# Two more staging buffers in the last projection stage, and a new order of GpSimd's and VectorE's work around the gate and up products

## The chip, the cores and the metric

The kernel runs on one core of one Trainium2 chip. Its time is the device time of one execution in microseconds (us); the time of a kernel is the median of its runs. The profile is one further execution, recorded by the hardware profiler. Its rows use these names: PE is TensorE's matmuls and PEld its weight loads, DVE is VectorE, ACT is ScalarE, POOL is GpSimd, SP is SyncE; SPq, ACTq and POOLq are the queues on which these engines issue transfers (DMA). `L115` is line 115 of the kernel before.

## The reference

The input x has 2048 rows of 640 columns. It is normalised by rows, goes through a local attention and, beside it, through a gated feed-forward without activation, and the two are joined:

```python
xn = _layernorm(x, axis=-1)
# attention: 32 heads of 20, each position looks at 8 positions, 2 apart, to its left
qkv = (xn @ wqkv)...
logits = einsum("bhsd,bhswd->bhsw", q, kg) * scale   # masked where the position is negative
o = einsum("bhsw,bhswd->bhsd", softmax(logits), vg)
s = o.reshape(B, S, D) @ wo
# feed-forward: 640 -> 1536 -> 640
h = (xn @ w_gate) * (xn @ w_up)
g = silu(h @ w_down)
out = x + s * g
```

All of it is float32.

## The kernel before

**Precision.** Each float32 operand of a matmul is held as two parts, a high part (ScalarE copies the value to the matmul's rounded type, L114) and a low part (value minus high part, L115, on GpSimd or VectorE; L1168, L829 and L975 are the same step elsewhere). Every product is the sum of three: high by high, high by low, low by high (`ALL3`). `split` makes both parts.

**Stages.** The text of the program is one long list, unrolled; each engine works through its own instructions in the order in which they stand, and waits where an operand isn't there or a buffer isn't free.

1. Normalise and transpose x into `xT`, four pieces of 512 rows (tag `xc`), high and low part.
2. Queries, keys and values. `qkv` (L434) makes one tile of 128 rows with 15 matmuls, in one of three PSUM banks in turn (`q`, `g`, `u`); ScalarE copies it to a staging buffer (L448), and after every second tile ScalarE's queue stores the buffer to DRAM (L452, `qkv_scr`). The heads are made in five passes (`MADE`); the last has 16 tiles, n = 0 to 15. `staged` holds three staging buffers: two halves of one slot `y` and one buffer `pk`; after n = 9 (`NT - 7`) the buffer `pk` leaves the list, because the high and low parts of the gate weights (`G`) go there next.
3. The attention itself runs on VectorE (L542, L549, L508 and the softmax, L564 to L578), GpSimd (the sums L514) and a little ScalarE, in the background of stages 2 and 4. It is a generator: `advance(budget)` adds to a credit, and steps of the attention are written into the program as long as the credit is positive, each at an assumed cost. In stage 4 the budget of a product is the number of its matmuls times `GROUP_RATE`. Finished heads are stored to `o_scr` (L590).
4. Gate and up. The 1536 columns of the two weights make 12 pieces f = 0 to 11 of 128. Pieces 1 to 11 are made in `group`: a 2 x 2 block scheme with seven products instead of eight, for two row pieces (`c0` and `c0 + 1`) and for gate and up at once. I write 1H, 2H and so on for `group(f, 2)`, the upper half of the rows, and 2L, 3L, ... for `group(f, 0, 1)` or, for f = 11, `group(f1)`, the lower half. The order is 1H, 2H, 2L, 3H, 3L, ..., 10H, 10L, 11L; the upper half of f = 11 follows as plain products (`gate` and `up`, L124).
5. The output projection, the down projection and the join.

**One group.** The seven products stand in the order j = 0, 5, 2, 1, 4, 3, 6 (steps n = 0 to 6) with 6, 9, 6, 9, 6, 9, 9 matmuls (L1310). A product reads one weight unit and one row unit. The weight units lie in four tiles that exist once: `G` (the gate: A11, A12 and a fifth, steps 0 and 1), `S` (the sums S1 to S3, steps 2, 3 and 4), `R` (S4 and the difference d5, step 5, and rows 3 to 5, which the split `U` fills: the up weight's A22, step 6, and its fifth, the last three matmuls of step 3 and of step 6). So, while group f runs, the tiles for f + 1 are written one after the other as their last readers finish: `w_add` makes the sums S1, S2, S3, S4, d5 on GpSimd (L1256), and `w_split` splits G, S, R, U (L114 on ScalarE, L115 on GpSimd). The dictionaries `one_places` (for f = 1) and `two_places` say at which step each of these stands: the key is (0 or 1 for the half, n). The raw weights come by `load_wf` (`wraw`, L180).

Row units named T1 to T4 are sums and differences of `xT`. Those for the upper half are made in stage 2. Those for the lower half were made early and stored; `load_t(0)` to `load_t(3)` (L1149, `t_scr`, 768 KB each) bring back four tiles of them. In the order of the units, T1 lies in tiles 0 and 1, T2's high part in tile 1, T2's low part in tile 2, T3 in tiles 2 and 3. T4 is written into the first rows of `xT` itself by `load_e` (L1153, `e_scr`, 512 KB each); `load_e(3, 0, 2)` and `load_e(3, 1, 3)` put the high and the low part of `xT[3]` back for the plain products of f = 11. All these transfers are issued by GpSimd, in the order of its instructions.

**The end of a group.** `hold(j)` (L1279, ScalarE) copies the bank after steps 0, 2, 3 and 4 (j = 0, 2, 1, 4) to tiles `gh`; the bank of j = 0, 2, 4, 6 is one and goes on accumulating, as does the bank of j = 1 and 3, so the next product on a bank waits for the copy. Then `gate_a` (L1292), `gate_b` (L1282) and `up_a` (L1295) on VectorE and `up_b` (L1285) and `h_b` (L1288) on `eng` finish gate and up and multiply them. `eng` is VectorE for the upper half from f = 2 on, and GpSimd otherwise. `gate_b` and `up_b` stand behind step 6's matmuls; `up_a` and `h_b` stand in `unfinished`, which the next group empties after its step 0 (`finish_piece`). The results are stored by SP (`store_h`, L1268).

**The last group.** The dictionary `beside` puts the first work of the output projection between the steps of 11L: `turn_pair(0)` (L725, L952 to L955), `hi_pair` (L971) and `lo_pair` (L975). After it come `gate(f1, 2)`, `up(f1, 2)`, `gate(f1, 3)`, `up(f1, 3)`. `up(f1, 2)` writes the bank that 11L used for j = 0, 2, 4, 6, so it waits for `up_a`.

Of the kernel before, what the change touches and what calls it, by code (L numbers as in the profile page):

```python
# [44 lines left out]
PACE = 1.0  # L45
VEC = 2
EARLY = 1
GROUP_RATE = 0.184


def tile_column(s):
# [5 lines left out]
def kernel(  # L57
# [702 lines left out]
    def wd_sum(n):  # L760

        t = {name: w_scr[:, i] for i, name in enumerate(("T1", "T2", "T3", "T4"))}
        if n == 0:
            for name, b in (("T1", "B11"), ("T3", "B12"), ("T2", "B22"), ("T4", "B21")):
                nc.sync.dma_start(t[name], wd_block(b))
        else:
            out, y = ((t["T1"], wd_block("B12")), (t["T3"], wd_block("B22")), (t["T2"], t["T1"]), (t["T4"], t["T2"]))[n - 1]
            nc.gpsimd.dma_start(out, y, accum_op=ALU.add)
# [188 lines left out]
    def hi_pair(p, part):  # L957

        if part == 2:
            z, raw = slot([P, 2, 3 * KS, P]) if p else blocks(w_big[0], 1, 2, 3 * KS), pair_raw[p]  # L960
        else:
            raw = pair_y[p][:, part]
            if p < 2:
                z = blocks(w_big[3], 3 + 2 * part, 2, KD) if p else blocks(w_kv["T2"], 1 + 2 * part, 2, KD)
            elif part == 0:
                z = blocks(w_big[p % 2], 2, 2, KD)
            else:
                z = slot([P, 2, KD, P]) if p % 2 else st([P, 2, KD, P], "pk", 1, F32R)
        z = [z[:, i] for i in range(2)]
        pair_z[p, part] = z, raw  # L970
        nc.scalar.activation(z[0], raw, AF.Copy)  # L971

    def lo_pair(p, part):
        z, raw = pair_z[p, part]
        nc.vector.tensor_sub(z[1], raw, z[0].bitcast(F32))  # L975
# [170 lines left out]
    def load_t(n):  # L1146

        tt[0].append(slot([P, 3, CH]))
        nc.gpsimd.dma_start(tt[0][n], t_scr[:, 3 * n:3 * n + 3])  # L1149

    def load_e(ch, a, n):

        nc.gpsimd.dma_start(xT[ch][a][:, 0:2, :], e_scr[n])  # L1153
# [93 lines left out]
    def w_add(f, *names):  # L1247

        if f not in w_sum:
            w_sum[f] = st([P, 9, P], "wraw", 2)  # L1250
        r, t = wf_raw[f], w_sum[f]
        v = {"A11": r[:, 0:2, 0], "A12": r[:, 2:4, 0], "A21": r[:, 0:2, 1], "A22": r[:, 2:4, 1], "g5": r[:, 4, 0],
             "u5": r[:, 4, 1], "S1": t[:, 0:2], "S2": t[:, 2:4], "S3": t[:, 4:6], "S4": t[:, 6:8], "d5": t[:, 8]}
        for name in names:
            a, b = W_SUM[name]
            nc.gpsimd.tensor_tensor(v[name], v[a], v[b], op=ALU.add if name == "S1" else ALU.subtract)  # L1256
# [14 lines left out]
    def group(f, c0=0, second=0):  # L1271

        b = {"A": pt([P, CH], "g", 2), "C": pt([P, CH], "u", 2), "B": q_one}
        kept, later = {}, []
        eng = nc.vector if c0 and f >= VEC else nc.gpsimd

        def hold(j):
            kept[j] = st([P, CH], "gh", 5)
            nc.scalar.activation(kept[j], b["ACACABA"[j]], AF.Copy)  # L1279

        def gate_b():
            nc.vector.tensor_add(kept[2], kept[2], b["C"])  # L1282

        def up_b():
            eng.tensor_add(kept[1], kept[1], kept[4])  # L1285

        def h_b():
            eng.tensor_mul(kept[2], kept[2], kept[1])  # L1288
            store_h(f, c0 + 1, kept[2])

        def gate_a():
            nc.vector.tensor_add(kept[0], kept[0], b["B"])  # L1292

        def up_a():
            nc.vector.tensor_mul(kept[0], kept[0], b["A"])  # L1295
            store_h(f, c0, kept[0])

        if not second:
            if not two(f - 1):
                w_split(f, "U")  # L1300
            w_sum.pop(f, None)
            wf_raw.pop(f)
        for n, j in enumerate((0, 5, 2, 1, 4, 3, 6)):
            y = b["ACACABA"[j]]
            runs = [(w_unit(f, H_IN[j], k)[i], x_in(W_IN[j], l, k, c0)) for i, l in ALL3 for k in range(2)]
            if j in FIVE:
                name, ch = FIVE[j]
                runs += [(w_unit(f, name)[i], xT[c0 + ch][l][:, KD - 1, :]) for i, l in ALL3]
            for r, (w, x) in enumerate(runs):
                nc.tensor.matmul(y, w, x, start=j in (0, 1, 5) and r == 0, stop=r == len(runs) - 1,  # L1310
                                 skip_group_check=True)
            if j in (0, 1, 2, 4):
                hold(j)
            finish_piece()
            if n == 6 and (second, n) in places and (second or f == F_TWO):
                places.pop((second, n))(f)
            for act in later:
                act()
            later = {5: [gate_a], 3: [gate_b, up_b]}.get(j, [])
            if j == 6:  # L1320
                unfinished.extend([up_a, h_b])
            if (second, n) in places:
                places[second, n](f)
            if (f, second, n) in beside:
                beside[f, second, n]()
            if (second, n) == (0, 0) and f < f1 and f + 1 not in wf_raw:
                load_wf(f + 1)
            advance(PACE * len(runs) * (GROUP_RATE if two(f) else 0.184))
# [38 lines left out]
        yield  # L1367

    steps += [differences(k) for k in range(2)]
    paced = 0.0  # L1370
    last, BLOCK = len(MADE) - 1, (3, 4, 6, 8, 10)
    W_SUMS = ((1, 2), (1, 12), (2, 4), (2, 12), (3, 7))
    RATE = ((1.0, 0.4), (0.3, 0.2), (0.4, 0.6), (0.8, 0.8))
    for m, t in ((m, t) for m in range(1, len(MADE)) for t in range(DIL)):
        r = t if m < last else DIL - 1 - t
        begin_unit(m, r)
        heads, broad = MC[m] // DH, m < last and MC[m + 1] > CMAX
        for i in range(NE):
            n = t * NE + i
            if 1 < m < last and n == 0:  # L1380
                load_wq(m + 1, ((0, 3), (3, 5)))
            if m < last and n in BLOCK:
                split_wq(m + 1, nc.gpsimd, (BLOCK.index(n), BLOCK.index(n) + 1))
            elif broad and n == BLOCK[1] + 1:
                load_wq(m + 1, ((4, 5),))
            if (m, r, i) == (last - 1, 1, 6):
                load_wf(F_TWO)
            if (m, n) in W_SUMS:
                wd_sum(W_SUMS.index((m, n)))
            qkv(m, r, i)  # L1390
            if m == last and n == NT - 7:
                staged[:] = [y for y in staged if y is not stage_pk[-1]]
            elif m == last and n == NT - 5:
                load_t(0)
            elif m == last and n == NT - 3:
                w_split(F_TWO, "G")
            if i == 1:
                finish_piece()
            advance(PACE * heads * 0.38)
            paced += RATE[m - 1][t]  # L1400
            while paced >= 1:
                paced -= 1
                step()
        if (m, r) == (last - 1, 1):
            steps.append(first_parts())
        elif (m, r) == (last, 1):
            for k in range(2):
                last_difference(k)
# [13 lines left out]
    def sums(*names):  # L1422
        return lambda f: w_add(f + 1, *names)

    def splits(*names):
        return lambda f: w_split(f + 1, *names)
# [2 lines left out]
                  (1, 2): splits("G"), (1, 4): splits("S"), (1, 5): splits("R"), (1, 6): splits("U")}  # L1429

    def load_late(n):
        if n == 0:
            load_t(1)
            load_t(2)
        elif n == 1:
            load_t(3)
        else:
            load_e(1, 0, 0)
            load_e(1, 1, 1)

    one_places = {(0, 1): sums("S1", "S2"), (0, 2): sums("S3", "d5", "S4"), (0, 3): splits("G"), (0, 4): splits("S"),
                  (0, 5): splits("R"), (0, 6): splits("U")}
    for f in range(F_TWO, f1):
        places.clear()
        places.update(two_places if f > F_TWO else one_places)
        if f == F_TWO:
            places[0, 0] = lambda f: load_late(0)
            places[0, 2] = lambda f: (load_late(1), w_add(f + 1, "S3", "d5", "S4"))
        elif f == F_TWO + 1:
            places[0, 0] = lambda f: load_late(2)  # L1450
        group(f, 2)
        if f > F_TWO:
            group(f, 0, 1)
    places.clear()
    beside.update({(f1, 0, 0): lambda: split_wo(1, nc.vector),
                   (f1, 0, 2): lambda: (turn_pair(0), load_pair(1)), (f1, 0, 4): lambda: (hi_pair(0, 0), lo_pair(0, 0)),
                   (f1, 0, 6): lambda: (hi_pair(0, 1), lo_pair(0, 1), load_e(3, 1, 3)), (f1, 0, 5): sum_w5,
                   (f1, 0, 3): lambda: load_e(3, 0, 2)})
    group(f1)
    finish_piece()  # L1460
    begin_wd()
    begin_wd()
    hi_pair(0, 2)
# [191 lines left out]
```

## Time and profile before

| | |
|---|---|
| median of 3 runs | 744.15 us (741.97 to 746.37) |
| profiled execution | 743.58 us, of which the recorded span is 741.8 us |
| PE busy | 729.6 us, 98% of the span |
| DVE busy | 627.2 us, 85% |
| POOL busy | 444.4 us, 60% |
| ACT busy | 305.9 us, 41% |

The last passes of queries, keys and values end, and group 1H begins, at 260.47 us of the span; 11L begins at 498.30 us. A row of the timeline gives start and duration, engine, line, operation, output tile <- input tiles and how many instructions are merged in it; square brackets give the idle time of the engine just before the row, and what ended it. A row of the waits gives who waited for whom: total us, times, longest us. Where the engine that a bracket names had long been done, it was another, often a transfer.

### The profile page before, as it was taken

How to read it: one execution, taken by the hardware profiler on the slowest of the kernel's cores; microseconds unless marked ns; L12 is line 12 of the kernel's file. 1: busy time of each engine (PE TensorE's matmuls, PEld its weight loads, DVE VectorE, ACT ScalarE, POOL GpSimd, SP SyncE). 2: the span in 40 equal slices, each digit the busy share in tenths (PEclk: the TensorE clock that was granted, in tenths of full speed). 3: DMA queues.
4: the chain of work that ended last, by engine and by line, in shares of the span. 5: the costliest groups of instructions: out<-in, count | busy, mean ns of one | idle time of the engine just before them, and what ended most of it. 6: DMA issues, size and time to landing. Idle time of an engine off the chain costs nothing. (4 is left out here: it accounts for less than half of the span.)

```text
span 741.8 us, 11069 instructions
## 1 busy us (share of the span) xinstructions
PE 729.6 (98%) x4024; PEld 664.4 (90%) x4024; DVE 627.2 (85%) x740; ACT 305.9 (41%) x568; POOL 444.4 (60%) x383
## 2 busy tenths in 40 slices
PE   8999999999999999999999999999999999999997
PEld 6989999888999977788888888887999999999997
DVE  7676989998868888899999998977899997777775
ACT  5668333222331332233224332335465664444442
POOL 6159937495959887988798969865744640000000
PEclk9999999999999999999999999999999999999999
DMA  8464799977493695544634462348777865555534
GB/s 322 168 202 162 254 335 326 267 211 221 159 261 90 202 315 173 155 124 154 182 119 126 148 167 66 88 155 216 201 231 234 306 243 192 192 192 192 192 107 141
DMA packets 106580, 144.44 MB, mean 195 GB/s; under 512 B 23096, under 2 KB 75572, under 8 KB 106526
## 3 DMA queue, kind: packets, MB, share of 16 engines
q1 hardware_dynamic: 88798, 121.78, 51.5%
q10 hardware_dynamic: 16000, 12.78, 5.4%
q0 software_dynamic: 1728, 9.18, 5.2%
q8 instruction: 31, 0.51, 0.3%
q14 instruction: 23, 0.19, 0.1%
HBM read 95.05 MB, written 55.67 MB: 203 GB/s over the span
## 5 line engine op out<-in xcount | busy, mean ns | idle before, releaser
L514 POOL TENSOR_TENSOR o<-o,t 128x960 f32<-128x960 f32 (+1 forms) x66 | 133.5, 2023 | 10.8 <-DVE t L508 9.9
L508 DVE TENSOR_TENSOR t<-e,kv 128x960 f32<-128x960 f32 (+1 forms) x96 | 99.8, 1039 | 23.5 <-POOL o L514 23.4
L542 DVE TENSOR_TENSOR t<-q,kv 128x1920 f32<-128x1920 f32 (+1 forms) x48 | 92.5, 1927 | 2.4 <-ACT s L1165 2.3
L549 DVE TENSOR_REDUCE lg<-t 128x96 f32<-128x1920 f32 (+1 forms) x48 | 92.3, 1924 | 0.2
L434 PE MATMUL q<-s,xc 128*128 128x360 f32 (+1 forms) x450 | 83.0, 334 | 1.9 <-ACT s L448 1.1
L115 POOL TENSOR_TENSOR s<-wraw,s 128x384 fp32r<-128x384 f32 (+6 forms) x60 | 71.3, 1202 | 22.4 <-ACT s L114 22.4
L1279 ACT ACTIVATE gh<-g 128x512 f32<-128x512 f32 x60 | 35.9, 599 | 115.6 <-PE g L1310 107.0
L434 PEld LDWEIGHTS q<-s,xc 128*128 128x128 f32 x450 | 74.9, 188 | 6.1 <-ACT s L448 1.4
L434 PE MATMUL u<-s,xc 128*128 128x360 f32 (+1 forms) x360 | 65.8, 334 | 0.0
L1310 PE MATMUL u<-xc,s 128*128 128x512 f32 x240 | 61.8, 391 | 0.9 <-POOL s L115 0.8
L434 PEld LDWEIGHTS u<-s,xc 128*128 128x128 f32 x360 | 60.3, 188 | 2.3
L434 PE MATMUL g<-s,xc 128*128 128x360 f32 (+1 forms) x330 | 61.5, 337 | 0.0
L1310 PE MATMUL g<-s,s 128*128 128x512 f32 x240 | 61.0, 389 | 0.0
L434 PEld LDWEIGHTS g<-s,xc 128*128 128x128 f32 x330 | 55.7, 188 | 2.6
L866 PE MATMUL q<-xc,s 128*128 128x320 f32 x342 | 55.5, 309 | 0.0
L1310 PEld LDWEIGHTS u<-xc,s 128*128 128x128 f32 x240 | 44.9, 188 | 11.7 <-POOL s L115 1.7
L1310 PEld LDWEIGHTS g<-s,s 128*128 128x128 f32 x240 | 45.0, 188 | 9.3
L866 PEld LDWEIGHTS q<-xc,s 128*128 128x128 f32 x342 | 51.5, 188 | 0.0
L114 ACT ACTIVATE s<-wraw 128x384 fp32r<-128x384 f32 (+6 forms) x61 | 34.7, 584 | 33.9 <-PE g L1310 10.4
L1310 PE MATMUL g<-xc,s 128*128 128x512 f32 x180 | 44.4, 391 | 0.8 <-ACT gh L1279 0.8
L1310 PE MATMUL q<-xc,pk 128*128 128x512 f32 x180 | 44.1, 389 | 0.0
L1310 PEld LDWEIGHTS g<-xc,s 128*128 128x128 f32 x180 | 33.6, 188 | 8.8 <-ACT gh L1279 1.9
(344 smaller groups left out, 1524.9 us busy)
## 6 DMA issues: line engine op xcount, KB each, us to landing
h_scr<-gh SPq DMA_DIRECT2D x48, 256.0 KB, 2.6
wraw<-in_wgu SPq DMA_DIRECT2D x12, 640.0 KB, 4.6
kv<-qkv_scr SPq DMA_DIRECT2D x14, 480.0 KB, 5.9
t<-h_scr SPq DMA_DIRECT2D x8, 768.0 KB, 5.9
qkv_scr<-s ACTq DMA_DIRECT2D x17, 360.0 KB, 5.9
kv<-qkv_scr SPq DMA_DIRECT2D x14, 367.5 KB, 6.3
s_scr<-gh SPq DMA_DIRECT2D x16, 320.0 KB, 3.9
gh<-s_scr SPq DMA_DIRECT2D x16, 320.0 KB, 4.0
```

The lines of the kernel that those rows point to most:

```text
L114: nc.scalar.activation(hi, raw, AF.Copy)
L115: eng.tensor_sub(lo, raw, hi.bitcast(F32))
L434: nc.tensor.matmul(p, xT[(r * NE + i) // TPC][a][:, k, t0:t0 + P], wq[m][b][k], start=n == 0, stop=n == len(runs) - 1, skip_group_check=ac ...
L508: nc.vector.tensor_mul(t.rearrange("p (n d) -> p n d", d=DH), e[:, :, w].unsqueeze(2).to_broadcast([P, NE * nh, DH]), v)
L514: return NE * c * cost, lambda: eng.tensor_add(y, z, t)
L542: nc.vector.tensor_mul(t, q, k)
L549: nc.vector.tensor_reduce(out=lg[:, :, j:j + 2].rearrange("p n a -> p a n"), in_=t.rearrange("p a (n d) -> p a n d", d=DH), op=ALU.add, ax ...
L866: nc.tensor.matmul(p, y[:, i, k], wd_part(name, k, l), start=new and r == 0, stop=r == len(runs) - 1, skip_group_check=True)
L1279: nc.scalar.activation(kept[j], b["ACACABA"[j]], AF.Copy)
L1310: nc.tensor.matmul(y, w, x, start=j in (0, 1, 5) and r == 0, stop=r == len(runs) - 1, skip_group_check=True)
```

## The change

There are six parts.

- **Staging.** At n = 0 of the last pass a second slot of two staging buffers (`more`) joins `staged`, which then has five; after n = 9 they leave it again together with `pk`.
- **Rate.** `GROUP_RATE` goes from 0.184 to 0.187: steps of the attention come a little earlier in the groups.
- **`h_b` behind `up_b`.** Where `eng` is GpSimd (1H and all lower halves), `h_b` and its store stand directly behind `up_b`, after step 6 of the same group, and no longer behind `up_a` of the next.
- **Group 2's weights.** In 1H, the split G moves from step 3 to step 2, ahead of all sums; S1, S2 and S3 stand at step 3; S stays at step 4; d5 and S4 stand at step 5, ahead of the split R; U stays at step 6.
- **Loads.** `load_t(1)` stays at step 0 of 1H; `load_t(2)`, `load_t(3)` and the two `load_e` stand at steps 0, 2 and 4 of 2H. Before, `load_t(2)` stood behind `load_t(1)`, `load_t(3)` at step 2 of 1H and the two `load_e` at step 0 of 2H.
- **The last low part.** `lo_pair(0, 1)` moves from step 6 of 11L to behind that group's `finish_piece`, that is behind `up_a`.

```diff
-GROUP_RATE = 0.184
+GROUP_RATE = 0.187
...
-            later = {5: [gate_a], 3: [gate_b, up_b]}.get(j, [])
+            later = {5: [gate_a], 3: [gate_b, up_b] + [h_b] * (eng is nc.gpsimd)}.get(j, [])
             if j == 6:
-                unfinished.extend([up_a, h_b])
+                unfinished.extend([up_a] + [h_b] * (eng is nc.vector))
...
-    paced = 0.0
+    paced, more = 0.0, []
...
+            if m == last and n == 0:
+                y = slot([P, 2, 2 * 3 * CMAX], F32)
+                more.extend([y[:, 0], y[:, 1]])
+                staged.extend(more)
             qkv(m, r, i)
             if m == last and n == NT - 7:
-                staged[:] = [y for y in staged if y is not stage_pk[-1]]
+                staged[:] = [y for y in staged if all(y is not z for z in more + [stage_pk[-1]])]
+                more.clear()
             elif m == last and n == NT - 5:
                 load_t(0)
...
     def load_late(n):
-        if n == 0:
-            load_t(1)
-            load_t(2)
-        elif n == 1:
-            load_t(3)
+        if n < 3:
+            load_t(n + 1)
         else:
             load_e(1, 0, 0)
             load_e(1, 1, 1)
 
-    one_places = {(0, 1): sums("S1", "S2"), (0, 2): sums("S3", "d5", "S4"), (0, 3): splits("G"), (0, 4): splits("S"),
-                  (0, 5): splits("R"), (0, 6): splits("U")}
+    one_places = {(0, 2): splits("G"), (0, 3): sums("S1", "S2", "S3"), (0, 4): splits("S"),
+                  (0, 5): lambda f: (w_add(f + 1, "d5", "S4"), w_split(f + 1, "R")), (0, 6): splits("U")}
...
         if f == F_TWO:
             places[0, 0] = lambda f: load_late(0)
-            places[0, 2] = lambda f: (load_late(1), w_add(f + 1, "S3", "d5", "S4"))
         elif f == F_TWO + 1:
-            places[0, 0] = lambda f: load_late(2)
+            for n, at in enumerate((0, 2, 4), 1):
+                places[0, at] = lambda f, n=n: load_late(n)
         group(f, 2)
...
-                   (f1, 0, 6): lambda: (hi_pair(0, 1), lo_pair(0, 1), load_e(3, 1, 3)), (f1, 0, 5): sum_w5,
+                   (f1, 0, 6): lambda: (hi_pair(0, 1), load_e(3, 1, 3)), (f1, 0, 5): sum_w5,
                    (f1, 0, 3): lambda: load_e(3, 0, 2)})
     group(f1)
     finish_piece()
+    lo_pair(0, 1)
```

## The prediction

> **What bounds the kernel now.** I read the page first, for the engines' shares, then the waits of TensorE, then its timeline.
>
> ```profile
> PE 729.6 (98%) x4024; PEld 664.4 (90%) x4024; DVE 627.2 (85%) x740; ACT 305.9 (41%) x568; POOL 444.4 (60%) x383
> ```
>
> TensorE works nearly without a break, and the change takes no matmul away. So only its gaps can be won, and they have to be found one by one:
>
> ```profile
> 237.47 2.56 PE L434 MATMUL g<-s,xc 128*128 128x360 f32 x15
> 239.87 2.56 PE L434 MATMUL u<-s,xc 128*128 128x360 f32 x15
> 243.56 0.75 PE L434 MATMUL q<-s,xc 128*128 128x360 f32 x3 [1.13 <-ACT s L448]
> ...
> 272.71 1.07 PE L1310 MATMUL g<-xc,pk 128*128 128x512 f32 x4
> 275.24 0.73 PE L1310 MATMUL g<-xc,pk 128*128 128x512 f32 x2 [1.46 <-POOL pk L115]
> 282.02 0.50 PE L1310 MATMUL u<-xc,s 128*128 128x512 f32 x1 [0.80 <-POOL s L115]
> 283.90 2.34 PE L1310 MATMUL u<-xc,s 128*128 128x512 f32 x9
> 286.67 2.33 PE L1310 MATMUL g<-xc,s 128*128 128x512 f32 x9 [0.43 <-ACT gh L1279]
> 288.84 1.52 PE L1310 MATMUL g<-xc,pk 128*128 128x512 f32 x6
> 301.08 1.52 PE L1310 MATMUL g<-xc,pk 128*128 128x512 f32 x6
> 314.70 1.52 PE L1310 MATMUL g<-xc,pk 128*128 128x512 f32 x6
> ...
> 510.66 3.56 PE L124 MATMUL g<-xc,pk 128*128 128x512 f32 x15
> 515.39 3.74 PE L124 MATMUL g<-xc,s 128*128 128x512 f32 x15 [1.18 <-DVE gh L1295]
> ```
>
> Start to start is the measure, since it holds the restart too. A tile of the last pass takes 2.40 us (237.47 to 239.87); the one that should follow comes after 3.69, **1.3 lost**. Group 2L, undisturbed, takes 12.24 us (288.84 to 301.08), or 0.2267 for each of its 54 matmuls. 2H takes 16.13 (272.71 to 288.84), **3.9 lost**; 3H 13.62, **1.4 lost**. From 314.70 to 510.66 sixteen groups take 16 x 12.25: nothing to win. The product at 510.66 needs 15 x 0.2267 = 3.40, and the next starts after 4.73, **1.3 lost**. Together 7.9 us: more than that this change can't bring.
>
> **Staging buffers: 0.** The bracket at 243.56 names a copy of ScalarE. What held it?
>
> ```profile
> 238.32 1.01 SPq L590 DMA_DIRECT2D o_scr<-o  x2
> 242.42 0.52 ACTq L452 DMA_DIRECT2D qkv_scr<-s  x1
> 242.50 1.54 POOL L514 TENSOR_TENSOR o<-t 128x640 f32<-128x640 f32 x1 [1.69 <-DMA o_scr<-o]
> ```
>
> The store of the pair leaves ScalarE's queue (L452) only at 242.42, 2.55 us after TensorE began the tile at 239.87, and the copy stands behind that store. So it is the store's issue that waits, not a buffer; and at 242.50 GpSimd is released by the landing of `o_scr`, issued at 238.32. I read that the store waits for that same transfer, which no third or fifth buffer moves. Gain 0; 1.3 if I read it wrongly, or if the order of the queues comes out otherwise. The new slot costs nothing: it is one that the pass before has left, and `load_t(0)` takes it two tiles after `more` leaves the list.
>
> **Group 2's weights: 0.8 gained, not 2.6.** GpSimd's durations, from the groups of its instructions between 264 and 290 us:
>
> ```profile
> L514 POOL TENSOR_TENSOR o<-o,t 128x640 f32<-128x640 f32 x6 | 9.4, 1561 | 0.1
> L115 POOL TENSOR_TENSOR s<-wraw,s 128x768 fp32r<-128x768 f32 x1 | 1.8, 1837 | 0.0
> L115 POOL TENSOR_TENSOR pk<-wraw,pk 128x640 fp32r<-128x640 f32 x1 | 1.5, 1530 | 0.0
> L1256 POOL TENSOR_TENSOR wraw<-wraw 128x256 f32<-128x256 f32 x2 | 1.5, 748 | 1.2 <-DMA wraw<-in_wgu 1.2
> ```
>
> The gaps in the list are next to nothing: in this stretch GpSimd is the bound, and an order can't shorten it, only loads that leave it can. Before, it runs like this:
>
> ```profile
> 264.29 1.11 POOL L1149 DMA_DIRECT2D s<-t_scr x2
> 280.98 0.99 POOL L115 TENSOR_TENSOR s<-wraw,s 128x384 fp32r<-128x384 f32 x1
> 281.94 1.28 POOL L1285 TENSOR_TENSOR gh<-gh,gh 128x512 f32<-128x512 f32 x1
> 283.18 1.56 POOL L514 TENSOR_TENSOR o<-o,t 128x640 f32<-128x640 f32 x1
> 284.71 1.28 POOL L1288 TENSOR_TENSOR gh<-gh,gh 128x512 f32<-128x512 f32 x1
> ```
>
> The low part of U at 280.98 is what TensorE waits for at 282.02. After, from 264.29: one load (0.56), two attention sums with VectorE's product between (to 268.8); G's high part needs the raw weights, which land by 268.15 (below), so G's low part runs 268.9 to 270.4; S1 to S3 (3 x 0.74) to 272.6; a sum to 274.15; S to 276.0; d5 and S4 (1.2), then ScalarE's high part (0.5), then R (1.0) to 278.7; a sum to 280.2; U to **281.2**, against 281.97. G is in time: wanted 4 matmuls into 2H, 273.6. But the wait moves on to U, wanted after 29 matmuls, 279.3. TensorE passes that point 0.8 earlier than now. The bounds are 0 (GpSimd no faster) and 2.7 (no wait left there).
>
> A wait is added too. ScalarE's high part of G now stands ahead of the copy of step 3:
>
> ```profile
> 267.47 0.60 ACT L1279 ACTIVATE gh<-u 128x512 f32<-128x512 f32 x1 [1.44 <-PE u L1310]
> 268.15 0.74 ACT L114 ACTIVATE pk<-wraw 128x640 fp32r<-128x640 f32 x1
> ```
>
> GpSimd waited 1.2 us for the raw weights (the list's last row) and ScalarE took them at 268.15; the split can't start before they land, and the copy behind it slips from 267.47 to 268.8. Step 5's product waits for that copy: up to 0.9 us, in 1H. It costs nothing, because the wait for U takes it up; without that cover it is 0.9.
>
> **`h_b` behind `up_b`: 0.7 in 2H, and 3H's 1.4.** At 283.18 a sum of the attention stands between the two multiplies, and ScalarE's copy before 286.67 wants a `gh` buffer that `h_b` frees. Without the sum `h_b` ends 1.5 earlier; 283.90 to 286.67 is 2.77 where nine matmuls need 2.04: 0.7 gained (0 at the least). Group 3's weights wait for a load behind `h_b`'s store on SP:
>
> ```profile
> 286.49 0.46 SPq L180 DMA_DIRECT2D wraw<-in_wgu  x1
> 293.85 0.74 POOL L1256 TENSOR_TENSOR wraw<-wraw 128x256 f32<-128x256 f32 x1 [3.55 <-DMA wraw<-in_wgu]
> ```
>
> With `h_b` 2.2 earlier this load and GpSimd's chain for 3H are some 2 us earlier too, and 3H's loss goes: 1.4 (0.7 if only the pattern around `h_b` goes). `up_a`'s store now stands behind `h_b`'s on SP; its buffer is next wanted several us later.
>
> **The loads: 0.8 lost.** `load_t(2)` now stands behind `h_b` and a sum: 281.2 + 1.28 + 1.28 + 1.55 = 285.3. 2H gains 1.5, so 2L starts at 287.3, and T2's low part is wanted 17 matmuls later, 291.2: 5.9 us. Issue to landing of the four loads before, least, median, most:
>
> ```profile
> DMA to landing us min/median/max: 5.4/8.0/11.1
> ```
>
> Bounds: 0 late and 5.2 late. The load is alone in its queue now, where two went out together at 264.29; so I take the middle of least and median, 6.7: 0.8. `load_t(3)`, 2.2 later, has 7.4 us left, the `load_e` about 8: in time.
>
> **The end: 1.3 gained, 1.8 lost.**
>
> ```profile
> 509.75 0.58 POOL L1153 DMA_DIRECT2D xc<-e_scr  x1
> 514.15 1.72 POOL L1288 TENSOR_TENSOR gh<-gh,gh 128x512 f32<-128x512 f32 x1 [3.82 <-issue]
> ```
>
> ```profile
> 513.92 0.82 DVE L975 TENSOR_TENSOR kv<-wraw,kv 128x640 fp32r<-128x640 f32 x1
> 514.66 0.68 DVE L1295 TENSOR_TENSOR gh<-gh,g 128x512 f32<-128x512 f32 x1
> ```
>
> `up_a` (L1295) takes the low part's place at 513.92 and ends at 514.6; TensorE wants it at 514.06. VectorE also comes earlier by itself. It waits for TensorE 2.8 us at `gate_b` before the last groups,
>
> ```profile
> DVE gh L1282 <- PE u L1310: 1.5, 2, 0.9
> DVE gh L1282 <- issue: 1.3, 2, 0.9
> ```
>
> and the higher rate (0.003 x 54 = 0.16 us of credit a group) puts attention steps there. With fewer waits for GpSimd I take 3.5, and TensorE 2.1 earlier: VectorE 1.4 earlier beside it. So that wait goes: 1.3.
>
> But in 11L GpSimd's `load_e(3, 1, 3)`, issued at 509.75 now, comes behind `h_b`, which waits for `gate_b` (L1282): 514.15 + 1.28 = 515.4, less 1.4: 514.0. It brings the low rows of `xT[3]`, wanted by the sixth matmul of `gate(f1, 3)`: 510.66 + 35 x 0.2267 = 518.6.
>
> ```profile
> DMA to landing us min/median/max: 5.2/6.4/7.7
> ```
>
> These are the two such loads of this stretch. At 6.4 it lands at 520.4, **1.8 late**; bounds 0 (5.2, VectorE 3.5 earlier) and 4.
>
> **Sum.** 0 - 0.8 - 0.7 - 1.4 + 0.8 - 1.3 + 1.8 = -1.6 us. The profiled execution took 743.58, so 742.0; the median of the runs lies 0.57 above that execution: **742.5**.
>
> **The rivals.**
>
> *The loads are in time* (no 0.8, no 1.8): -4.2, median 739.9. For it: landings of 5.4 and 5.2 were seen. Against it: both medians, 8.0 and 6.4, are longer than the room, 5.9 and 4.6. The Trainium skill ("DMA: Bandwidth & Descriptors", section "Anatomy of one DMA — SWDGE (gpsimd) path") puts a transfer from GpSimd at 2.0 us plus bytes at 436 GB/s, an estimate of 3.8 us for 768 KB; by that rule both loads are in time and the time is this rival's. The six landings here, 5.2 to 11.1, are all longer.
>
> *A late T2, slower than before.* In 2L the load lands after 11.1, as one of four did: 5.2 lost instead of 0.8, +2.8, median 746.9. It decides from a landing of 8.2 on: then its loss outweighs the rest. For it: the raw weights of group 3 (286.49 now) go out just ahead. Against: the 11.1 was one of two loads issued together.
>
> *The stores are freed as well*: 1.3 more, 741.2.
>
> *GpSimd is no faster*, the change does nothing for U, and 3H keeps half: -0.7 - 0.7 + 0.8 + 0.5 = -0.1, 744.0.
>
> **Chances.** Forecast 0.40 (its own range 740.8 to 744.5), loads in time 0.27, stores freed 0.08, late T2 0.13, GpSimd no faster 0.12. Half a per cent, 3.7 us, is about what a measurement of this kernel can tell from no change: faster means below 740.4, which most of the second case and some of the first and third give, 0.30; slower, above 747.9, is the far part of the late load, 0.07; the same 0.63. Range 738.8 to 746.0.
>
> **What would show it.** The wait at 243.56 stays. TensorE's bracket for `pk` in 2H is gone and the one for `s` (U) stays, at 281 and not 282. Waits before T2 in 2L and before the sixth matmul of `gate(f1, 3)`, with transfers as releasers, are the two losses; if TensorE's waits show neither, the loads were in time and the forecast is wrong by 2.6. If U comes before 279.3, my chain of GpSimd is wrong.

## The result, and the profile after

The changed kernel takes **755.75 us** (median of 4 runs, 754.80 to 757.39), against 744.74 us for the kernel before in the same comparison: a ratio of 1.0154, 95% interval 1.0118 to 1.0190. It is 11 us slower, where 742.5 was forecast; the forecast's range ended at 746.0, its slowest rival at 746.9. The rival that was slower, a late T2, is not what happened either: the four loads of T land after 5.3 to 7.4 us and TensorE never waits for one.

The page of the changed kernel, its span and first part:

```profile
span 753.0 us, 11070 instructions
PE 733.7 (97%) x4024; PEld 666.7 (89%) x4024; DVE 630.2 (84%) x740; ACT 305.2 (41%) x568; POOL 444.3 (59%) x383
```

The counts of the engines' instructions are the same; the span is 11.2 us longer. Next the waits of TensorE in the changed kernel (in all, times, longest):

```profile
PE g L1310 <- ACT gh L1279: 5.5, 3, 2.7
PE u L1310 <- POOL s L115: 2.5, 2, 1.5
PE u L124 <- DMA xc<-e_scr: 2.0, 1, 2.0
...
PE g L1310 <- POOL pk L115: 0.4, 1, 0.4
```

The wait of 1.46 for `pk` in 2H is gone (the 0.4 in the last row lies in 6H), and the load at the end (third row) is late, as forecast. The first row has grown: in the kernel before it is 0.8 us in two waits of at most 0.4. Where it lies, TensorE's timeline says:

```profile
240.37 2.56 PE L434 MATMUL u<-s,xc 128*128 128x360 f32 x15
244.07 2.74 PE L434 MATMUL q<-s,xc 128*128 128x360 f32 x15 [1.14 <-ACT pk L448]
...
273.81 1.52 PE L1310 MATMUL g<-xc,pk 128*128 128x512 f32 x6
275.17 2.20 PE L1310 MATMUL q<-xc,pk 128*128 128x512 f32 x9
279.65 2.31 PE L1310 MATMUL g<-s,s 128*128 128x512 f32 x6 [2.27 <-ACT gh L1279]
281.76 2.50 PE L1310 MATMUL u<-s,s 128*128 128x512 f32 x6
284.10 0.86 PE L1310 MATMUL u<-xc,s 128*128 128x512 f32 x3
...
290.25 1.52 PE L1310 MATMUL g<-xc,pk 128*128 128x512 f32 x6
302.49 1.52 PE L1310 MATMUL g<-xc,pk 128*128 128x512 f32 x6
316.23 1.52 PE L1310 MATMUL g<-xc,pk 128*128 128x512 f32 x6
...
428.76 1.52 PE L1310 MATMUL g<-xc,pk 128*128 128x512 f32 x6
430.12 2.20 PE L1310 MATMUL q<-xc,pk 128*128 128x512 f32 x9
435.05 1.66 PE L1310 MATMUL g<-s,s 128*128 128x512 f32 x6 [2.73 <-ACT gh L1279]
...
520.37 3.56 PE L124 MATMUL g<-xc,pk 128*128 128x512 f32 x15
524.36 3.69 PE L124 MATMUL g<-xc,s 128*128 128x512 f32 x15 [0.43 <-DVE gh L1295]
...
531.20 2.56 PE L124 MATMUL u<-xc,pk 128*128 128x512 f32 x10 [2.01 <-DMA xc<-e_scr]
```

Read start to start, against 12.24 us for a group. 2H takes 16.44 (273.81 to 290.25), 3H 13.74. The fifteen groups from 3L up to the start of 11L, at 508.02, take 191.79 us, where 15 x 12.24 = 183.60 would do and the kernel before takes just that (314.70 to 498.30): **8.2 us** lost in a stretch in which nothing had been lost. The four products from `gate(f1, 2)` on take 16.6 instead of 15.1. In the table, "lost" is time beyond 12.24 us a group, or beyond 13.6 (4 x 15 x 0.2267) for the four products; every number comes from the starts in the profiled run. The medians of the runs, and the ratio to the kernel before in the same comparison, stand beside. In e1, e4, e9 and e14 the profiled run lost a further 2.7 to 3.6 us in the projection stage, in e7 1.8; in e1, e4, e7 and e14 a landing of `o_scr` at 217 us, ahead of all that was edited, came 1.1 to 1.5 us later. The columns leave this out, the medians may hold some of it (e4's median is its profiled run).

The first column scatters by itself. The edit of e13 begins behind 2H, so up to there it is the kernel before a second time: its 2H takes 15.31 us, not 16.13, and the wait for `pk` is 0.63, not 1.46. In e2, e6 and e7, which change the rate but neither the order of group 2's weights nor the place of `h_b`, 2H takes 15.2 to 15.4. A difference of 0.8 us in 2H between two profiles is therefore no effect yet.

| kernel | 1H to 3H | 3L to 10L | four products | median us, ratio (95%) |
|---|---|---|---|---|
| before | 5.3 | 0.0 | 1.5 | |
| changed | 5.8 | 8.2 | 3.0 | 755.75, 1.0154 (1.0118 to 1.0190) |
| e1 changed, rate 0.184 | 5.7 | 4.0 | 4.7 | 751.92, 1.0113 (1.0083 to 1.0143) |
| e2 before, rate 0.187 | 3.9 | 6.7 | 1.5 | 750.70, 1.0090 (1.0068 to 1.0112) |
| e3 changed, `h_b` old | 7.7 | 6.8 | 0.5 | 753.00, 1.0128 (1.0101 to 1.0155) |
| e4 before, `h_b` new | 3.6 | 2.9 | 2.9 | 749.25, 1.0072 (1.0045 to 1.0099) |
| e5 changed, both undone | 7.7 | 0.0 | 0.5 | 746.15, 1.0035 (1.0019 to 1.0052) |
| e6 before, rate 0.181 | 3.4 | 9.5 | 0.0 | 751.52, 1.0115 (1.0088 to 1.0142) |
| e7 e2 with one add moved | 4.4 | 4.7 | 1.5 | 749.47, 1.0076 (1.0049 to 1.0102) |
| e8 before, two parts | 4.2 | 0.0 | 0.7 | 743.34, 0.9996 (0.9980 to 1.0011) |
| e9 changed, 7L's steps later | 5.6 | 7.9 | 3.3 | 755.74, 1.0163 (1.0132 to 1.0194) |
| e10 changed, sums early | 5.3 | 8.5 | 4.1 | 755.74, 1.0156 (1.0134 to 1.0178) |
| e11 before, three parts | 4.6 | 0.0 | 0.8 | 743.55, 0.9995 (0.9979 to 1.0011) |
| e12 e2, nine adds on GpSimd | 6.0 | 8.7 | 0.4 | 752.80, 1.0122 (1.0095 to 1.0150) |
| e13 before, nine adds on GpSimd | 7.5 | 5.3 | 1.5 | 752.04, 1.0116 (1.0088 to 1.0145) |
| e14 changed, load first | 5.7 | 7.9 | 0.0 | 754.30, 1.0136 (1.0098 to 1.0173) |

### The profile page after: what moved, and what is told of

Read it like the earlier page. It is cut to its first block, busy times and chain, and to the rows that moved or that the text cites. A ratio compares the mean times of both kernels' runs of the same rounds, so it can differ in the third digit from the quotient of the medians.

```text
span 753.0 us, 11070 instructions
## 1 busy us (share of the span) xinstructions
PE 733.7 (97%) x4024; PEld 666.7 (89%) x4024; DVE 630.2 (84%) x740; ACT 305.2 (41%) x568; POOL 444.3 (59%) x383
## 4 chain that ended last, share of the span: by engine, by line
PE 64%; POOL 13%; DVE 9%; DMA 6%; issue 5%; SPq 1%; ACT 1%; ACTq 0%; POOLq 0%; DVEq 0%
PE q L866 8%; PE q L434 8%; POOL o L514 7%; PE u L434 6%; PE u L866 6%; PE g L434 5%; PE g L1310 4%; PE u L124 4%; PE u L1310 3%; DMA o_scr<-o 3%; PE q L996 3%; PE g L866 3%; PE e L866 3%; PE g L124 3%; PE u L996 2%
## 5 line engine op out<-in xcount | busy, mean ns | idle before, releaser
L1279 ACT ACTIVATE gh<-g 128x512 f32<-128x512 f32 x60 | 35.8, 597 | 104.9 <-PE g L1310 98.0
L1310 PE MATMUL g<-s,s 128*128 128x512 f32 x240 | 62.9, 397 | 5.9 <-ACT gh L1279 5.5
L1310 PEld LDWEIGHTS u<-xc,s 128*128 128x128 f32 x240 | 44.8, 188 | 13.6 <-POOL s L115 3.3
L514 POOL TENSOR_TENSOR o<-t 128x960 f32<-128x960 f32 (+1 forms) x11 | 22.1, 2009 | 35.6 <-DVE t L508 23.7
```

Source lines behind the costliest of these rows:

```text
L514: return NE * c * cost, lambda: eng.tensor_add(y, z, t)
```

## The experiments

**The two suspects, each undone and each alone (e1 to e5).** The diffs, one line for each run:

```diff
 # e1, on the changed kernel (e2: the other way, on the kernel before)
-GROUP_RATE = 0.187
+GROUP_RATE = 0.184
 # e3, on the changed kernel (e4: the other way, on the kernel before; e5: e1 and e3 together)
-            later = {5: [gate_a], 3: [gate_b, up_b] + [h_b] * (eng is nc.gpsimd)}.get(j, [])
+            later = {5: [gate_a], 3: [gate_b, up_b]}.get(j, [])
-                unfinished.extend([up_a] + [h_b] * (eng is nc.vector))
+                unfinished.extend([up_a, h_b])
```

> The changed kernel with the old GROUP_RATE 0.184, all else as changed. The changed kernel takes 755.75 us (median), the one before 744.74. Of the 11.2 us more, 8.2 are lost from 3L to 10L, where the forecast put nothing: 3L 0.8, 6H 1.4, 8H 3.0, 9H 2.4, small ones 0.6. Theory RATE: the higher rate moves attention steps ahead of ScalarE's copies and GpSimd's splits there, and this is where the 8.2 come from: about 747.5 us, and groups from 314 to 510 us at 12.24 us again. Theory H_B: GpSimd's h_b, now ahead of the attention's sum, delays the sums and all that waits for them: about 755, with the stalls in 6H, 8H, 9H still there. Theory BOTH: either one alone would be harmless, only the two together overload: about 747, but then each alone on the kernel before costs nothing.

> The kernel before with GROUP_RATE 0.187 and nothing else. RATE: about 753 us (744.7 + 8.2), with TensorE waiting in groups 3L to 10L. H_B: 744.7. BOTH: 744.7.

> The changed kernel with h_b back in the list of unfinished work for all groups (behind the attention steps of the last product), rate 0.187. RATE: about 755, stalls in 6H, 8H and 9H still there. H_B: about 747.5. BOTH: about 747.

> The kernel before with GpSimd's h_b right behind up_b, rate 0.184, the rest as before. RATE: 742.5 to 745 (the forecast's 0.7 in 2H and up to 1.4 in 3H gained; 11L's load behind h_b up to 2 lost). H_B: about 752. BOTH: 744.7.

> The changed kernel with both the old rate 0.184 and h_b at its old place: what is left are the staging buffers, the order of group 2's weights, the loads one by one, and the low part behind the last product. Theory TWO CAUSES (only the rate and h_b cost): 742.5 to 743.5, the old time less the 1.0 that the run with the old h_b won between gate(f1, 2) and the product behind it (14.1 us there instead of 15.1), and no wait from 3L to 10L. Theory ORDER (each shift on GpSimd, whatever it is, meets VectorE's multiplies and adds of two buffers elsewhere, and they wait until GpSimd pauses): 746 to 750; undoing the rate gave 3.8 and undoing h_b 2.8 of 11.2, so some 4.6 would stay, with waits in groups that none of the remaining edits touches.

The column "3L to 10L" answers. On the kernel before: the rate alone costs 6.7, `h_b` alone 2.9, neither 0. On the changed kernel: rate undone 4.0, `h_b` undone 6.8, both undone 0.0, both left 8.2. So each costs by itself, and together they cost less than their sum: BOTH is false, and RATE and H_B each hold a part; neither holds the whole, as each had been put, and no time of e1 to e4 is the one that either named. What is left in e5 loses nothing from 3L on, so ORDER, which had waits in groups that none of the remaining edits touches, is false, although e5's 746.15 lies in the range given for it and above the 742.5 to 743.5 of TWO CAUSES: the loss of e5 is in 1H to 3H (7.7 instead of 5.3), partly paid back at the end. In 3H it isn't VectorE's doing either: TensorE waits 1.56 us for U there, and ahead of that GpSimd stood still for 2.39, until a landing of `o_scr` at 299.94.

The rate's first damage is done in 5L and paid for in 6H. GpSimd's and then VectorE's timeline in e2, where 5L begins at 362.35:

```profile
361.76 0.73 POOL L1256 TENSOR_TENSOR wraw<-wraw 128x256 f32<-128x256 f32 x1
...
366.49 0.73 POOL L1256 TENSOR_TENSOR wraw<-wraw,wraw 128x256 f32<-128x256 f32 x1
372.18 2.27 POOL L514 TENSOR_TENSOR o<-o,t 128x960 f32<-128x960 f32 x1 [4.96 <-DVE t L508]
```

```profile
362.17 0.68 DVE L1282 TENSOR_TENSOR gh<-gh,u 128x512 f32<-128x512 f32 x1
362.77 5.01 DVE L1285 TENSOR_TENSOR gh<-gh,gh 128x512 f32<-128x512 f32 x1
```

`up_b` (L1285) takes 5.01 us, while `gate_b` (L1282) just before it, of the same size but with one operand in PSUM (`u`), takes 0.68. `up_b` has both operands in SBUF. It ends at 367.78, 0.56 after GpSimd's unbroken run of five sums of weights and one of the attention ends (361.76 to 366.49 + 0.73 = 367.22). Then GpSimd in its turn stands still for 4.96, waiting for VectorE's products. GpSimd's split of the next weights is behind that, and TensorE pays in 6H.

**One such add moved (e7), all of them moved (e12, e13).**

```diff
 # e7, on e2; e12 (on e2) and e13 (on the kernel before) have nc.gpsimd there for every group
-            eng.tensor_add(kept[1], kept[1], kept[4])
+            e = nc.gpsimd if (f, c0) == (5, 2) else eng
+            e.tensor_add(kept[1], kept[1], kept[4])
```

> The kernel before with rate 0.187, and up_b of 5H (one instruction) on GpSimd instead of VectorE. At rate 0.187 alone (750.7 us) this instruction takes 5.01 us on VectorE (0.68 where nothing is beside it), while GpSimd works without a break; the next sums of GpSimd wait 4.96 us for VectorE, and 6H takes 14.98 us instead of 12.24. Theory PORT (VectorE waits, with two operands in SBUF, until GpSimd pauses): VectorE is 4.3 us earlier there, 6H takes 12.3 to 12.8, and the kernel 748 to 748.5, although GpSimd has 1.28 us more to do. Theory LOAD (GpSimd has too much to do by the earlier steps, the long add is only its sign): 6H takes 14.98 plus up to 1.28, and the kernel 751 to 752.

> The kernel before with rate 0.187, and up_b of every H group from 2H on on GpSimd (h_b stays on VectorE), so that nine of the adds that VectorE was held in leave it and GpSimd gets 9 x 1.28 us more. At rate 0.187 alone VectorE's instructions of lines 1285 and 1288 take 14.2 us more than their 0.68 each from 3L to 10L, and TensorE loses 6.7 there. Theory PORT: the surplus falls below 7 and the loss below 3 us. Theory LOAD (the loss is GpSimd's excess of work by the earlier steps): the loss rises to 7 or more.

> The same at the old rate 0.184, as the control: the kernel before loses 0.0 from 3L to 10L with a surplus of 4.9. PORT: surplus 2 to 4, loss 0 to 1, kernel 743 to 745. LOAD: loss of 2 or more. Theory ALIGNMENT (each shift loses, whatever its kind): loss 3 to 8 in both runs.

In e7 the same stretch of VectorE's timeline (its line numbers are one higher from `h_b` on):

```profile
364.85 2.15 DVE L549 TENSOR_REDUCE lg<-t 128x96 f32<-128x1920 f32 x1
...
368.08 3.02 DVE L1289 TENSOR_TENSOR gh<-gh,gh 128x512 f32<-128x512 f32 x1 [0.49 <-POOL gh L1286]
```

The reduce, which started 5.35 us behind the start of 5L in e2 (367.70 - 362.35), stands 0.43 behind it (5L begins at 364.42 here), and 6H takes 13.03 instead of 14.98, although GpSimd has 1.28 us more to do. That is against LOAD, which had at least 14.98, and mostly with PORT, which had 12.3 to 12.8. It is not the whole of it: now the multiply (L1289) takes 3.02 beside GpSimd's next run, and the kernel's 749.47 lies in the range of neither and moves by no more than the runs scatter. Moving all nine adds went the other way. VectorE's multiplies then wait for GpSimd's adds; the waits of VectorE in e12:

```profile
DVE gh L1288 <- POOL gh L1285: 16.4, 8, 3.7
```

The surplus (VectorE's time on these lines beyond 0.68 each, from 3L to 10L) did fall in e12, from 14.2 to 5.5 us, since the adds are no longer VectorE's; at the old rate it rose, from 4.9 to 8.2. The loss rose in both, from 6.7 to 8.7 and from 0.0 to 5.3. By the numbers set beforehand that speaks for LOAD or ALIGNMENT and against PORT alone; but the 16.4 us of new waits come from the move itself, so these two runs don't isolate the port. Its share in the 8.2 stays open.

**The rate on the other side (e6).**

```diff
-GROUP_RATE = 0.184
+GROUP_RATE = 0.181
```

> The kernel before with GROUP_RATE 0.181, as far below the old rate as the changed one is above it. Theory EARLY (attention steps placed earlier than at 0.184 cost): 743 to 745, no wait from 3L to 10L. Theory ALIGNMENT (0.184 is a placement at which VectorE's two-buffer adds happen not to meet GpSimd's long runs, and a shift to either side loses): 747 to 751, with an add or multiply of line 1285 or 1288 on VectorE of over 2.5 us somewhere and a wait of TensorE within 15 us after it.

As far below as the change went above, it loses 9.5 us, nearly all in two groups: EARLY is false, and of ALIGNMENT the first half holds, that a shift to either side loses. Its second half does not: the two places, 3L and 10L, have no such add in the 15 us before them. 3L has a queue. ScalarE, then TensorE, in e6:

```profile
317.53 0.39 ACT L571 ACTIVATE e<-lg 128x256 f32<-128x256 f32 x1 [6.34 <-DVE lg L569]
317.85 0.96 ACT L498 ACTIVATE q<-q 128x960 f32<-128x960 f32 x1
318.75 0.58 ACT L1279 ACTIVATE gh<-g 128x512 f32<-128x512 f32 x1
```

```profile
319.38 1.89 PE L1310 MATMUL g<-s,s 128*128 128x512 f32 x6 [2.32 <-ACT gh L1279]
```

The exponential of a new head (L571) waits for VectorE, and the copy of the group's first product (L1279), which TensorE needs two products later, stands behind it in ScalarE's queue. In the kernel before the two stand in the same order in 3L, but the exponential runs 0.78 us behind the group's start (315.48) and not 4.04, and costs nothing: at this place it is VectorE's lateness that changed, not the order. In 10L no head changes; there the copy waits 4.19 us for VectorE's add (L1285), which takes its usual 0.68 but starts only at 499.36, behind steps of the attention.

**The same queue in the changed kernel (e9, e10).** In 8H the order did change. ScalarE before, where the copy comes first, and in the changed kernel, where the exponential does and the copy follows at 434.42:

```profile
426.42 0.60 ACT L1279 ACTIVATE gh<-g 128x512 f32<-128x512 f32 x1 [1.06 <-PE g L1310]
427.81 0.50 ACT L571 ACTIVATE e<-lg 128x384 f32<-128x384 f32 x1 [0.79 <-DVE lg L569]
```

```profile
433.10 0.49 ACT L571 ACTIVATE e<-lg 128x384 f32<-128x384 f32 x1 [3.84 <-DVE lg L569]
```

```diff
 # e9
+            if (f, c0, n) == (7, 0, 6):
+                credit[0] += PACE * len(runs) * GROUP_RATE
+            else:
                 advance(PACE * len(runs) * (GROUP_RATE if two(f) else 0.184))
 # e10
-    one_places = {(0, 2): splits("G"), (0, 3): sums("S1", "S2", "S3"), (0, 4): splits("S"),
-                  (0, 5): lambda f: (w_add(f + 1, "d5", "S4"), w_split(f + 1, "R")), (0, 6): splits("U")}
+    one_places = {(0, 2): splits("G"), (0, 3): sums("S1", "S2", "S3", "d5", "S4"), (0, 4): splits("S"),
+                  (0, 5): splits("R"), (0, 6): splits("U")}
```

> The changed kernel; the attention steps that its rate puts behind the last product of 7L are taken one product later, behind the first product of 8H and its copy (no other step moves by the credit). In the changed kernel 8H takes 15.27 us, with TensorE waiting 2.73 us for ScalarE's copy of the first product, which stands behind the exponential of a new head, which waits 3.84 us for VectorE. Theory QUEUE (it is the exponential's place ahead of the group's first copy): 8H takes 12.3 to 13, and the kernel 753. Theory LATE VECTOR (VectorE is simply late there, whatever the order): 8H still takes about 15, or the loss turns up at the copies of the third or fourth product.

> The changed kernel with the sums d5 and S4 of group 2 back beside S1 to S3 (step 3 of 1H), the rest as changed. In the changed kernel 2H takes 16.44 us: TensorE waits 2.27 us for ScalarE's copy of the first product, which stands behind ScalarE's high part of R, which waits for GpSimd's d5 and S4. Theory QUEUE: R's high part is done before the copy is due, that wait goes, and S's low part comes 1.2 later: 2H takes 14 to 15.3, the kernel 754 to 755. Theory BOUND (GpSimd's sum of work sets 2H's end): 2H takes 16.4 whatever the order, with the wait at S or U.

In e9 TensorE's wait for that copy is gone, but a wait of 1.54 for GpSimd's U comes in its place, 8H takes 14.40, 9H 15.27 instead of 14.67, and the kernel 755.74. QUEUE is right that this wait hangs on the exponential's place, and wrong that the time comes back; LATE VECTOR is right that it does not, but neither had named U. In e10 2H takes 13.92 instead of 16.44, so QUEUE is right and BOUND wrong there: 2.5 us won, the largest gain of all runs in that group. And the kernel takes 755.74 again. TensorE's timeline in e10 shows who took them:

```profile
291.71 0.50 PE L1310 MATMUL g<-s,s 128*128 128x512 f32 x1 [0.50 <-DMA s<-t_scr]
...
309.03 0.50 PE L1310 MATMUL u<-xc,s 128*128 128x512 f32 x1 [1.55 <-POOL s L115]
...
433.99 2.50 PE L1310 MATMUL g<-s,s 128*128 128x512 f32 x6 [2.71 <-ACT gh L1279]
436.29 2.31 PE L1310 MATMUL u<-s,s 128*128 128x512 f32 x6
```

2L waits for the second T (the forecast's late load, now that 2L starts early enough: the bracket is 0.5, and 2L takes 13.05 us, 0.8 more than 12.24, just what the forecast had put), 3H takes 14.89. 8H and 9H together take 29.9 us in the changed kernel, 29.7 in e9, 30.3 in e10, 30.0 in e14, whatever was edited before them, and though their shares differ (8H 14.4 to 16.9): what TensorE wins early in that stretch it waits for later, so something else sets the pace there.

**Which engine sets the pace there.** VectorE is the nearest. Its busy time, the third engine of the row, in the fifteen groups, before and after:

```profile
314.70:498.30 183.60, 183.60 (x812) 152.03 (x810) 171.44 (x169) 60.97 (x102) 153.86 (x118) 1.00 0.45 131
```

```profile
316.23:508.02 191.79, 186.19 (x811) 151.37 (x810) 180.27 (x172) 60.75 (x101) 154.35 (x118) 1.00 0.43 126
```

VectorE works 171.4 of 183.6 us before, 93%, where the page says 85% for the whole span. After, it is busy 8.8 us longer, for a stretch that is 8.2 longer, and idle as little as before (11.5 and 12.2 us). Most of the 8.8 are the sixteen instructions with two operands in SBUF. Their groups before, then after:

```profile
L1288 DVE TENSOR_TENSOR gh<-gh,gh 128x512 f32<-128x512 f32 x8 | 9.4, 1172 | 0.0
L1285 DVE TENSOR_TENSOR gh<-gh,gh 128x512 f32<-128x512 f32 x8 | 6.4, 804 | 0.0
```

```profile
L1285 DVE TENSOR_TENSOR gh<-gh,gh 128x512 f32<-128x512 f32 x8 | 15.1, 1890 | 0.0
L1288 DVE TENSOR_TENSOR gh<-gh,gh 128x512 f32<-128x512 f32 x8 | 7.1, 893 | 0.0
```

15.8 us became 22.2, 6.4 more. In e5, which loses nothing, they take 15.6.

This makes VectorE likely, and doesn't show it. Other kernels lose time in the same groups although VectorE has more room there than before: it is idle for 15.8 of 193.1 us in e6, which loses 9.5, and for 19.1 of 188.9 in e13, which loses 5.3. So the amount of VectorE's work alone can't be the cause; when it gets to a step that others wait for counts too.

**The late load (e14).**

```diff
-            later = {5: [gate_a], 3: [gate_b, up_b] + [h_b] * (eng is nc.gpsimd)}.get(j, [])
+            later = {5: [gate_a], 3: [gate_b, up_b] + [lambda: load_e(3, 1, 3)] * (f == f1)
+                     + [h_b] * (eng is nc.gpsimd)}.get(j, [])
-                   (f1, 0, 6): lambda: (hi_pair(0, 1), load_e(3, 1, 3)), (f1, 0, 5): sum_w5,
+                   (f1, 0, 6): lambda: hi_pair(0, 1), (f1, 0, 5): sum_w5,
```

> The changed kernel with the load of the low rows of xT[3] ahead of h_b in 11L. The stretch from gate(f1, 2) to the product behind the four (13.6 us without a wait) takes 16.62 in the changed kernel, with a wait of 2.0 for that load. By the forecast's step the wait goes: 14.1 to 14.6, the kernel 753.5. If the load is late for another reason (the channel, not its place), 16 to 17 and 755.7.

The four products take 13.62 us, and the wait for `xc<-e_scr` is no longer among TensorE's waits; so the late load was a matter of its place. The 13.62 is below the 14.1 to 14.6 expected, since the wait for `up_a` is gone in this profile as well, which the edit doesn't explain. The kernel's 754.30 is within the scatter of 753.5.

**The parts that seemed good, alone (e8, e11).**

```diff
 # e8, on the kernel before; the move of lo_pair(0, 1) behind group(f1) as in the changed kernel, and
+            later = {5: [gate_a], 3: [gate_b, up_b] + [h_b] * (f == F_TWO)}.get(j, [])
+                unfinished.extend([up_a] + [h_b] * (f > F_TWO))
 # e11: e8 with e10's order of group 2's weights
```

> The kernel before with two of the changed kernel's parts: h_b behind up_b in group 1H alone, and the last low part behind the last product. By the parts as measured so far: 2H 14.8 instead of 16.1, 3H 13.3 instead of 13.6, the products from gate(f1, 2) on 14.1 instead of 15.1: 743.1 - 2.6 = 740.5 us. Theory ORDER: the sums behind 1H's multiply come later, and groups from 3L on lose it again as they do with h_b moved in all groups (3L 0.8, 10L 1.4): 742 to 744.

> The kernel before with h_b behind up_b in 1H alone, the last low part behind the last product, and G's split of group 2 ahead of all five sums (loads and rate as before). With the first two alone 743.3 us (743.34 to 744.13 of before, no difference). Theory QUEUE: 2H takes 13.5 to 14.8 and the kernel 741 to 742. Theory ORDER (whatever is shifted on GpSimd is paid for in 3H or later): 743 to 745.

In e8 2H takes 14.77 instead of 16.13 (or 15.31, as in e13) and the four products 14.27 instead of 15.1, 3H 13.90 instead of 13.6; nothing is lost from 3L on, against ORDER. The profiled run is 1.8 us shorter than that of the kernel before, but the medians differ by 0.8, and the interval holds 1: no difference that can be measured, and not the 740.5 expected. e11 is no better: its 2H takes 14.92, above the 13.5 to 14.8 of QUEUE. No kernel here beats the one before.

## Why the prediction was wrong

**The rate and `h_b` from 3L to 10L, the step that failed.** The forecast wrote "From 314.70 to 510.66 sixteen groups take 16 x 12.25: nothing to win", and gave the higher rate no term in its sum but an earlier VectorE at the end, and `h_b` none behind 3H. A stretch in which nothing can be won can still lose, and here it lost 8.2, where the rate alone loses 6.7 and `h_b` alone 2.9. A sign stood in the trace: in that stretch VectorE has 12 us of 184 to spare, not the 15% of the page. That rate and `h_b` are the two causes is shown (e1 to e5). How they work is shown at single places: a head's exponential ahead of a group's copy on ScalarE (8H, and 3L in e6), a two-operand add of VectorE held beside GpSimd (5L in e2 and e7). How the 8.2 divide between these two ways is not settled.

**Staging buffers, 0:** right. The tile takes 3.70 us (240.37 to 244.07), 3.69 before. The wait for `o_scr`, which I had inferred, stands in the trace of e1, on the copy behind the store on ScalarE:

```profile
244.40 0.47 ACT L448 ACTIVATE pk<-q 128x360 f32<-128x360 f32 x1 [5.54 <-DMA o_scr<-o]
```

**Group 2's weights, 0.8 gained:** wrong. GpSimd's chain came out as forecast: U's low part ended at 282.24, that is 281.2 and the 0.98 us by which 1H began later. The wait for G went, too. It did not move to U but to ScalarE's first copy of 2H. I had followed GpSimd's list alone: R's high part on ScalarE waits for GpSimd's d5 and S4, and the copy is queued behind it. ScalarE in the changed kernel:

```profile
278.18 0.94 ACT L114 ACTIVATE s<-wraw 128x384 fp32r<-128x384 f32 x2 [3.60 <-POOL wraw L1256]
279.02 0.58 ACT L1279 ACTIVATE gh<-g 128x512 f32<-128x512 f32 x1
```

I had named this very danger for G's high part in 1H, where it cost 0.1 (12.36), and not for R's. e10 shows it: 13.92. The 16.13 from which the gain was counted was itself high, as e13's 15.31 shows.

**`h_b`, 0.7 and 1.4:** half right. Alone (e4) 2H takes 1.3 less than in the kernel before, but only 0.5 less than in e13; 3H takes 0.3 less, not 1.4. In the later groups, where it now stands ahead of the attention's sums, 2.9 are lost; that the sums' delay is the way is argued, not shown. That it moves eleven multiplies, and not only the one of 2H that I costed, I left out. In the changed kernel neither gain arrives.

**The loads, 0.8 lost:** the condition didn't come about, since 2L started at 290.25 and not at 287.3. Where it does, TensorE waits for the second T: 2L loses 0.8 in e10 (in e3 1.2, in e5 0.5). The rule of the Trainium skill ("DMA: Bandwidth & Descriptors", section "Anatomy of one DMA — SWDGE (gpsimd) path") that the forecast cited for a rival, 3.8 us by its estimate, is not borne out: the landings after the change are again 5.3 us or more.

**The end:** that the load would be late was right (e14 takes it away); that it is 2.0 for the 1.8 forecast is in part luck, since it went out 4.7 us behind the start of `gate(f1, 2)` (525.07 - 520.37) and not 3.3, and TensorE's own remaining wait hid some of that. (The forecast's `h_b` of 1.28 us there is not its row's 1.72; after the change it took 1.29.) Of the 1.3 that the wait for `up_a` cost 0.7 went (520.37 to 524.36 is 3.99 us, 4.73 before): the low part that stood ahead of it is gone, but VectorE is no earlier by itself, as I had assumed; `gate_b` starts 2.66 us after `gate(f1, 2)` begins (523.03), 2.67 before.

The rest of the 11.2 us lies ahead of 1H: 0.5 because the profiled run reaches the last pass that much later, in the part of the program that the change doesn't touch, and 0.5 in slower matmuls behind the wait at 244.07 (2.47 us a tile, 2.40 before); e2, which shares neither the buffers nor the order, shows the same 2.47.

## What to carry to other kernels

Before a step is costed at nothing because a stretch has no wait, take the busy time of each engine in that stretch, not in the span: at 93% an engine that TensorE never waits for may be the next bound, and each order of the work is a placement that a shift in either direction can lose. When work is moved on one engine, follow each of its instructions into every queue that it feeds, since a copy behind a blocked one is late whatever it needs itself. A wait removed early is worth nothing until the engine that caused it has been followed to the end of the stage.

## What the hardware showed

**VectorE held beside GpSimd.** The 5.01 us above, for an add that takes 0.68, is the longest case; the changed kernel has the same 5.01 in the same group. The Trainium skill ("GPSIMD Engine Reference", section "1. Specifications") says that GpSimd's SBUF interfaces are shared with VectorE, with contention for VectorE's instructions that have two SBUF inputs. The trace agrees, and adds the size. What it does not show is that VectorE is held until GpSimd pauses. In the kernel before, GpSimd, then VectorE:

```profile
364.58 2.26 POOL L514 TENSOR_TENSOR o<-o,t 128x960 f32<-128x960 f32 x1 [0.27 <-DVE t L508]
366.79 1.62 POOL L1256 TENSOR_TENSOR wraw<-wraw 128x256 f32<-128x256 f32 x2
365.01 2.37 DVE L1288 TENSOR_TENSOR gh<-gh,gh 128x512 f32<-128x512 f32 x1
```

Here the multiply ends at 367.38, 0.54 us after GpSimd's sum (364.58 + 2.26 = 366.84), although GpSimd goes straight on; the next two sums of weights then take 1.62 instead of the 1.15 in e2. In the kernel before, in the changed one and in e2, 24 of these adds and multiplies take over 0.75 us from 3L to 10L, and each ends 0.54 to 0.56 us after the end of an instruction of GpSimd's. It need not be the next: in 5L of e2 four such ends went by first (at 364.7, 365.4, 366.1 and 366.5); why, no run here shows.

**TensorE's clock after a wait.** The granted clock (third number from the end) in the changed kernel, behind the wait in 2H and then behind the one in 8H:

```profile
279.60:282.00 2.40, 2.35 (x7) 1.91 (x8) 0.69 (x1) 0.01 (x1) 2.40 (x3) 0.67 0.00 0
282.00:284.20 2.20, 2.20 (x7) 1.71 (x7) 2.12 (x3) 0.59 (x1) 2.12 (x3) 0.59 0.02 4
...
435.00:437.60 2.60, 2.55 (x11) 2.13 (x12) 2.60 (x3) 0.60 (x2) 2.60 (x3) 1.00 0.00 0
```

From the modelled end of nine matmuls (275.17 + 9 x 0.2267 = 277.21) to 279.65 TensorE stood still for 2.44 us, and the next twelve matmuls take 4.45 us instead of 2.72: the wait of 2.4 costs 4.2. In 8H it stood still for 2.89 and nothing followed; in e10, at nearly the same place and for 2.87 us, the twelve matmuls behind it take 4.44. Read in the same way in all sixteen profiles, from start to start, TensorE stands still for 2.2 to 3.3 us twelve times in the groups; behind ten of these waits the next eighteen matmuls take 1.7 to 1.8 us more than 18 x 0.2267, behind two (2.89 here, 2.42 in e3) at most 0.2 more. The Trainium skill ("TensorE: Matmul & The Clock Gate", section "Why this matters for your kernels") asks for no gaps over some 3 us; here 2.2 (e1) was already too much, and 2.9 harmless once. What decides between them no run here shows.
